# Delta-rule attention with routed experts on one core: a tile for each PSUM bank, unread products that wait for rows, and a new order of all steps

## The chip, the core and the metric

The kernel runs on one core of a Trainium2 chip. Its engines are TensorE (PE, whose weight loads have a row of their own, PEld), VectorE (DVE), ScalarE (ACT), GpSimd (POOL) and SyncE (SP, which here issues most of the DMAs). The metric is the device time of one launch in microseconds (us). The time before is 541.99 us, the median of three runs (534.49, 541.99 and 543.96).

## What is computed

Two parts, one behind the other, all in float32:

```python
# attention, 4 x 8 heads, 768 steps, head size 48: a state of 48 x 48 per head
k_n = k / (norm(k) + 1e-6)
for t in range(768):
    y[t]  = q[t] @ state
    v_old = state.T @ k_n[t]
    state = state + beta[t] * outer(k_n[t], v[t] - v_old)
# experts: y is regrouped to x (3072 x 384); each row goes to one of 8 experts
e_idx  = argmax(x @ w_gate + modality_bias[modality_id])
out[i] = softmax_weight[i] * (relu(x[i] @ w1[e_idx]) @ w2[e_idx])      # hidden size 1024
```

## The kernel before

**Tiling.** The 768 steps are cut into 12 chunks `c` of 64 steps. A chunk has two groups `g` of heads, so there are 24 steps `i` = 2c+g. Within a chunk the recurrence is turned into matrix products: a gram matrix of the keys (`g{c}`, lines 182 to 194, copied out by `ev` and, for the first four chunks, by `dc`), the inverse of a triangular matrix made from it, and products with the state. The inverse is worked out row by row on DVE and POOL in three jobs; the first (`sub0_0` to `sub0_14`, lines 276 to 283) solves blocks of 16 for chunks 0 to 3, and `jy`, `ya`, `jx`, `r1`, `wt`, `mv` (lines 304 to 338) put blocks of 32 together from those of 16, for the eight steps 0 to 7: `jy` and `jx` are products on PE, `ya` copies one's result out for the other, `r1` adds on DVE. Then `y1`, `ys`, `r`, `rc` (lines 398 to 412) make the block of 64.

**The recurrence.** For each step i: `ks` (product of keys and state, line 437), `rh` (DVE subtracts it from the values, 439), `z` (product with the inverse, 443), `zt` (copied out in two halves by ACT or DVE), `ds` (state update in PSUM, 449), `sb` (state copied out), `qs` and `pz` (the output, 457 and 460), `xo` (copied out). Steps of one parity share a state in PSUM, S[0] or S[1].

**PSUM.** Four tiles of two banks each: S (the states), ZK (bank z for `z`, bank ks for `ks`), YG (bank y for `qs` and `pz`, bank gp for `y1`, `r` and small products), MO (two banks handed out to grams, transposes and the first expert's products). Where two engines touch one tile, the framework makes the later wait for the earlier by a semaphore; it does that by tile, so also where they touch different banks, and for two reads too.

**The order.** Every step is a named task of a plan; the string `ORDER` (line 28) lists the tasks in the order in which they are issued, a letter behind a number chooses the engine of a task that has a choice, and `in_order` (line 96) ties each engine to that order. So an engine whose next instruction waits holds up all that stands behind it, SP's DMAs too.

**Unread products.** `hf`, `hg`, `hx` (lines 374 to 379) are 46 products of 128x128 with 128 columns which nobody reads; they go to bank S[1]. Those of `hf` and `hg` are named after rows of the solve. `idle` and `gate` use `issue_after`, which orders instructions only on the engine of the instruction that it names. The rows are DVE's and the gated DMAs SP's, and the named instructions are not on the same engine as the work in the block, so in this kernel neither makes anything wait.

**Experts.** From about 309 us on, PE runs the experts' two layers, unit by unit, from prefetched weights. The first unit's first layer (`la_`, `lh`, `ll`) is part of the plan and stands at its end, on the banks of MO. The change doesn't touch the experts.

Of the kernel before, what the change touches and what calls it, by code (L numbers as in the profile page):

```python
# [49 lines left out]
590d 930d 931 230 991 231 232 233 932 928 933 998 1002 588 941 942 589d 907 904 935 999 934 592 944 936d 992 1000 1001 593 953 596d 908 938 993 955 995 946 945 996 943 594 954  # L50
939 595 909 1003 1004 948 997 1005 949 922 1006 1007 957 951 1008 1009 958 956 1010 1011 1012 952 1013 1014 1015 1016 1017 1020 1021 959 1018 1022 1019 1023 961 415 444 962 964
1024 1025 965 1026 950 966 1027 967 963 989 1028 960 947 968 937 1029"""

FILL="""\
"""

# [49 lines left out]
class Attention:  # L106
# [33 lines left out]
    def plan(s):  # L140
# [261 lines left out]
        def ys(i):  # L402
            t=s.tile("ys",i,[128,8,32],2)
# [647 lines left out]
```

## Time and profile before

| | before |
|---|---|
| time, median of 3 runs | 541.99 us |
| time of the profiled execution | 539.66 us |
| its span, first to last instruction | 537.9 us |
| PE busy | 469.1 us (87%) |
| DVE, ACT, POOL busy | 303.9, 220.8, 136.5 us |
| mean granted clock of TensorE | 0.882 |

The granted clock is a share of 2.4 GHz, and its two levels are 1.0 (2.4 GHz) and 0.5 (1.2 GHz); a value between them is a mean over a stretch. A row of a timeline gives the start, the duration, the engine, the line and what is written from what; "x10" merges ten records. PE leaves two records for a product of float32, so "x10" is five products. Brackets at a row's end name how long the engine had been idle and whose end released it.

### The profile page before, as it was taken

What the parts mean: (1) busy time and instruction counts of PE and PEld (TensorE: products, weight loads), DVE (VectorE), ACT (ScalarE), POOL (GpSimd) and SP (SyncE); (2) the same over time, 40 slices, a digit from 0 to 9 for tenths busy, and PEclk for the clock granted to TensorE, in tenths of its full rate; (3) what the DMA queues carried; (4) which work ended last, traced back from release to release, by engine and by line L of the source; (5) the groups of instructions that cost most, each with busy time, mean ns of one, the idle gap of its engine ahead of it and who ended that gap; (6) DMA issues with size and microseconds to landing.
All of it is one profiled execution on the core that took longest, in us unless ns stands there. A gap on an engine that the chain in (4) does not pass through costs nothing. (4 is left out here: it accounts for less than half of the span.)

```text
span 537.9 us, 16821 instructions
## 1 busy us (share of the span) xinstructions
PE 469.1 (87%) x7119; PEld 414.7 (77%) x7119; DVE 303.9 (56%) x647; ACT 220.8 (41%) x473; POOL 136.5 (25%) x176
## 2 busy tenths in 40 slices
PE   5755998988788897998897799999699999999994
PEld 5645787877667786877685579899489889899984
DVE  3895457497457477557354179955334535444630
ACT  5424344546266456552244263421232424333530
POOL 8007323466333261010300021104412213101121
PEclk9595556688799699997898999999799999999998
DMA  8688004476567376876520384523633533519701
GB/s 270 155 193 271 4 14 114 106 219 189 125 188 177 82 227 191 196 193 167 134 82 16 99 284 132 176 60 104 219 102 103 174 107 98 156 58 327 231 32 35
DMA packets 90628, 78.14 MB, mean 145 GB/s; under 512 B 49049, under 2 KB 78496, under 8 KB 90544
## 3 DMA queue, kind: packets, MB, share of 16 engines
q1 hardware_dynamic: 87408, 67.49, 44.3%
q0 software_dynamic: 3136, 9.49, 5.3%
q8 instruction: 58, 0.95, 0.7%
q14 instruction: 26, 0.21, 0.1%
HBM read 62.28 MB, written 14.73 MB: 143 GB/s over the span
## 5 line engine op out<-in xcount | busy, mean ns | idle before, releaser
L952 PE MATMUL opb<-w2hb,h 128*128 128x384 f32 x192 | 52.9, 340 | 0.5 <-DVE oob L955 0.5
L861 PE MATMUL hpb<-xh,w1xb 128*128 128x512 f32 x144 | 42.1, 405 | 0.6 <-ACT xh L826 0.6
L867 DVE SCALAR_TENSOR_TENSOR h<-hpb,h 128x512 fp32r<-128x512 f32 x24 | 16.6, 692 | 45.5 <-ACT h L865 45.5
L439 DVE TENSOR_TENSOR RHS<-vv,ZK 64x384 f32<-64x384 f32 x44 | 24.3, 551 | 21.6 <-PE ZK L437 6.5
L952 PEld LDWEIGHTS opb<-w2hb,h 128*128 128x128 f32 x192 | 34.8, 188 | 1.8 <-DVE oob L955 1.0
L865 ACT ACTIVATE h<-hpb 128x512 fp32r<-128x512 f32 x24 | 14.4, 598 | 51.0 <-PE hpb L861 51.0
L952 PE MATMUL opa<-w2ha,h 128*128 128x384 f32 x128 | 34.7, 343 | 0.3 <-ACT h L865 0.3
L346 POOL TENSOR_TENSOR tmx<-T,A 128x216 f32<-128x216 f32 (+12 forms) x23 | 18.4, 802 | 63.1 <-DVE T L347 62.5
L952 PE MATMUL opb<-w2lb,h 128*128 128x384 f32 x96 | 32.4, 338 | 0.0
L861 PEld LDWEIGHTS hpb<-xh,w1xb 128*128 128x128 f32 x144 | 27.5, 194 | 5.7 <-ACT xh L826 1.0
L25 ACT COPY Sb<-S 48x192 f32<-48x192 f32 x74 | 23.2, 313 | 18.2 <-PE S L721 6.8
L25 ACT COPY ZT<-ZK 64x384 f32<-64x384 f32 x41 | 19.4, 473 | 23.2 <-PE ZK L437 13.1
L449 PE MATMUL S<-ZT,kk 128*48 128x96 f32 x352 | 24.5, 292 | 4.3 <-issue 2.4
L460 PE MATMUL YG<-ZT,pb 128*64 128x96 f32 x384 | 24.4, 276 | 3.1 <-ACT ZT L25 1.3
L956 POOL DMA_INDIRECT out_dram<-oob,sidxb x12 | 12.2, 1016 | 57.8 <-DVE oob L955 29.5
L443 PE MATMUL ZK<-RHS,R 128*64 128x96 f32 x384 | 25.0, 282 | 1.9 <-DVE RHS L439 1.5
L414 POOL TENSOR_TENSOR vv<-vv,RR 128x384 f32<-128x384 f32 x18 | 15.7, 878 | 40.6 <-DMA kk<-in_kv_dram 26.5
L409 PE MATMUL YG<-R,ys 32*32 32x32 f32 x768 | 20.5, 207 | 5.9 <-issue 2.9
L25 ACT COPY R<-YG 32x256 f32<-32x256 f32 x44 | 15.9, 362 | 23.5 <-PE YG L409 13.5
L409 PEld LDWEIGHTS YG<-R,ys 32*32 32x32 f32 x768 | 17.2, 121 | 10.5 <-issue 4.8
L449 PEld LDWEIGHTS S<-ZT,kk 128*48 128x48 f32 x352 | 19.6, 150 | 6.0 <-issue 3.2
L146 ACT ACTIVATE ys<-YG 32x256 f32<-32x256 f32 x42 | 15.8, 375 | 20.6 <-PE YG L457 6.6
(372 smaller groups left out, 1193.2 us busy)
## 6 DMA issues: line engine op xcount, KB each, us to landing
kqr<-in_kq_dram SPq DMA_DIRECT2D x44, 256.0 KB
ke<-in_kq_dram SPq DMA_DIRECT2D x20, 256.0 KB
vv<-in_kv_dram SPq DMA_DIRECT2D x24, 192.0 KB
xd<-xo SPq DMA_DIRECT2D x24, 192.0 KB
w1rb<-in_moe_w_dram SPq DMA_DIRECT2D x12, 384.0 KB
w2rb<-in_moe_w_dram SPq DMA_DIRECT2D x12, 384.0 KB
kk<-in_kv_dram SPq DMA_DIRECT2D x22, 192.0 KB
w1ra<-in_moe_w_dram SPq DMA_DIRECT2D x8, 384.0 KB
```

Source lines behind the costliest of these rows:

```text
L25: if n=="scalar": nc.scalar.copy(o,i)
L146: if s.e=="ACT": A.activation(o,i,AF.Copy,scale=x)
L346: E[s.e].tensor_tensor(o,T[:,:,lo:lo+na,c:c+1].to_broadcast([128,n,na,nb]),X[:,:,c:c+1,c+1:32].to_broadcast([128,n,na,nb]),ALU.mult)
L409: for p in range(2): b=64*p; x=2*j+h; mm(o[b:b+32,x],s.ys[i][b+32:b+64,x],R[b+32:b+64,x,32:64],start=True,stop=True)
L414: if c: E[s.e].tensor_tensor(v,v,w,ALU.mult)
L439: c,g=divmod(i,2); b=64*p; V.tensor_tensor(s.RHS[g][b:b+64,:,48*p:48*p+48].rearrange("q (h j) c -> q h j c",h=2),s.KV[c,1][b:b+64,g],s.ks[ ...
L443: for h in range(2): mm(s.z[i][64*h:64*h+64,:,j,:],s.R[i%4][:,2*j+h,:],hc(s.RHS[i%2][:,4*h+j,:]),start=True,stop=True)
L449: for p in range(2): mm(o[64*p:64*p+48,j,:],K[:,4*p+j,:],s.ZT[g][:,4*p+j,:],start=False,stop=True,skip_group_check=True)
L460: for p in range(2): mm(s.y[i][64*p:64*p+64,:,j,:],s.PB[i//2][:,8*p+4*(i%2)+j],hc(s.ZT[i%2][:,4*p+j,:]),start=(i<2 and j==0),stop=True,ski ...
L861: if n in ks: mm=s.nc.tensor.matmul(hp[:,v,:],w[:,k,fs],x[:,k,0:T],start=(n==0),stop=(n==8))
L867: s.nc.vector.scalar_tensor_tensor(hl,hp,0.0,hh.bitcast(F32),ALU.max,ALU.subtract)
L952: mm=nc.tensor.matmul(op,h[:,f%nf,ts_],w[:,f%2,:],start=(n==0),stop=(n==23)); n+=1
```

## The change

Five edits, and a new table of numbers for the order of all 1030 tasks:

- **Banks.** The four tiles of two banks become eight tiles of one bank (S0, S1, z, ks, y, gp, MO0, MO1).
- **Unread products** go to bank y, which has no reader until the first `pz`, and must all be issued before `qs0`. Those tied to a row now wait for it by a semaphore (`gate` adds a wait to the first instruction of the block).
- **Gated DMAs.** The same `gate` now makes some early loads on SP wait for the gram products `g1` or `g3`.
- **`ya`** is split by bank: on ACT four instructions of 64 columns in place of two of 128, or two on DVE. The new order puts all eight on ACT.
- **`ys`**: one instruction over 128 rows in place of two over 32 rows (line 402).

```diff
-        S,ZK,YG,MO=(p.tile([128,1024],F32,name=n) for n,p in (("S",s.ps),("ZK",s.ps),("YG",s.ps),("MO",s.pm)))
-        h=lambda t: [t[:,512*g:512*g+512] for g in range(2)]
-        s.S=h(S); s.bk=dict(zip(("z","ks","y","gp"),h(ZK)+h(YG))); s.MO=h(MO); ...
+        B=lambda n,p: p.tile([128,512],F32,name=n)
+        s.S=[B(f"S{g}",s.ps) for g in range(2)]; s.bk={n:B(n,s.ps) for n in ("z","ks","y","gp")}; s.MO=[B(f"MO{g}",s.pm) for g in range(2)]; ...
         def gate(n,f):
-            with s.tc.issue_after(s.I[n].ins): f()
+            k=len(nc.cur_bb.bb.instructions); f(); i=nc.cur_bb.bb.instructions[k]
+            s.tc.add_manual_dep(i,s.I[n].name,mybir.DependencyInfo(mybir.DependencyClass.Sync,mybir.DependencyReason.DATA),reason="gate")
...
                 def ya(i):
-                    for b in range(2): mul(s.ya[:,i%2,:,:,32*b:32*b+16],s.jo[i][:,:,0:128].rearrange("q k (j b a) -> q k j b a",j=4,b=2)[:,:,:,b],s.mk[b])
+                    for p in range(2):
+                        o=s.ya[:,i%2,p].rearrange("q j (b a) -> q j b a",b=2)[:,:,:,0:16]; x=s.jo[i][p][:,0:128].rearrange("q (j b a) -> q j b a",j=4,b=2)
+                        if s.e=="DVE": V.tensor_tensor(o,x,s.cst[:,66:68].unsqueeze(1).unsqueeze(3).to_broadcast([128,4,2,16]),ALU.mult)
+                        else:
+                            for b in range(2): mul(o[:,:,b],x[:,:,b],s.mk[b])
...
         def idle(n,k=None):
-            with s.tc.issue_after(s.I[k]) if k else contextlib.nullcontext():
-                for _ in range(n): mm(s.S[1][:,384:512],s.ident,s.ident,start=2 not in s.gp,stop=True,skip_group_check=True)
-        for c in range(7,15): add(f"hf{c}","PE",.85,lambda c=c: idle(2,f"sub0_{c}"),[f"sub0_{c}","gf2"])
+            def f():
+                for _ in range(n): mm(s.bk["y"][:,384:512],s.ident,s.ident,start=False,stop=True,skip_group_check=True)
+            gate(k,f) if k else f()
+        fy=["gf1","gf5"]; fills=[f"hf{c}" for c in range(7,15)]+["hg0","hg1"]+[f"hx{n}" for n in range(24)]
+        for c in range(7,15): add(f"hf{c}","PE",.85,lambda c=c: idle(2,f"sub0_{c}"),[f"sub0_{c}",*fy])
...
-            for p in range(2): b=64*p+32; mul(t[b:b+32],s.lv[i][b:b+32,0:256].rearrange("q (x c) -> q x c",x=8),-1.0)
+            mul(t,s.lv[i][:,0:256].rearrange("q (x c) -> q x c",x=8),-1.0)
...
 ORDER="""\
-118 3 0 95 130 119 134a 131d 94 152 133d 120 92 93 122 156a 141 237 123 121d 99 155 96 243 124 144 97 98 132 135 1 8 163 101 153 238 2 154 145 239 172 240 164 165 9 112 143 241
+3 118 130 0 95 132d 133d 94 134a 119 93 123 152 131 92 121d 122 237 155 135 243 97 120d 156a 96 98 141 124 99 1 2 102 112 238 144 145 154 163 164 153 239 240 157 165 241 172
```

The order moves instructions in three places of which the prediction speaks.

**VectorE behind the first solve** (T is the solved matrix, W its two transposes, w1b the operand of `jy`, s and tt belong to the second job, A<-W is `r1`). Before:

```order
L285 TENSOR_TENSOR T_354<-T_354,t_450 128x1024 [waits DVE_49]
L288 STREAM_TRANSPOSE W_653<-T_354 128x16x32 [waits DVE_49]
L289 STREAM_TRANSPOSE W_653<-T_354 128x16x32
L288 STREAM_TRANSPOSE W_653<-T_354 128x16x32
L289 STREAM_TRANSPOSE W_653<-T_354 128x16x32
L254 RECIPROCAL tt_798<-s_701 128x64 [waits Activation_49]
```

and after:

```order
L282 TENSOR_TENSOR T_319<-T_319,t_418 128x1024 [waits DVE_49]
L285 STREAM_TRANSPOSE W_682<-T_319 128x16x32 [waits DVE_49]
L286 STREAM_TRANSPOSE W_682<-T_319 128x16x32
L143 TENSOR_SCALAR w1b_172<-W_682,cst 128x32x16 [waits DVE_49]
L285 STREAM_TRANSPOSE W_682<-T_319 128x16x32
L286 STREAM_TRANSPOSE W_682<-T_319 128x16x32
L143 TENSOR_SCALAR w1b_173<-W_682,cst 128x32x16 [waits DVE_49]
L143 TENSOR_SCALAR w1b_173<-W_682,cst 128x32x16
L322 SCALAR_TENSOR_TENSOR A_311<-W_682,cst,z 64x4x16 [waits PE_49,Activation_49]
```

Three of the four copies w1b move from ACT to DVE, and the first `r1` stands ahead of the second job's norm (the RECIPROCAL follows it now).

**ScalarE at the same place.** Before, the second job's square root (s, which waits for two DMAs) stands between the first two copies w1b:

```order
L146 ACTIVATE w1b_168<-W_653,cst 128x32x16 [waits DMAHW1_49,DVE_49]
L250 ACTIVATE s_701<-A_656,eps 128x64 [waits DMAHW5_49,DMAHW2_49]
L146 ACTIVATE w1b_168<-W_653,cst 128x32x16
L146 ACTIVATE w1b_169<-W_653,cst 128x32x16 [waits DVE_49]
L292 ACTIVATE A_339<-W_653,cst 128x32x16 [waits DVE_49,Activation_49]
```

and after, behind the first `ya`:

```order
L142 ACTIVATE w1b_172<-W_682,cst 128x32x16 [waits DMAHW7_49,DVE_49]
L289 ACTIVATE A_311<-W_682,cst 128x32x16 [waits DVE_49,Activation_49]
L142 ACTIVATE ya<-z,cst 128x4x16 [waits PE_49,Pool_49]
L142 ACTIVATE ya<-z,cst 128x4x16
L142 ACTIVATE ya<-ks,cst 128x4x16 [waits PE_49]
L142 ACTIVATE ya<-ks,cst 128x4x16
L247 ACTIVATE s_768<-A_618,eps 128x64 [waits DMAHW6_49,DMAHW4_49]
```

The square root and its wait no longer stand ahead of work that PE waits for. On PE, 16 unread products and 13 groups of small products (`jy`, `jx`, `y1`, `r`) then stand between the first `jy` and the first `z`. Of the ten groups of unread products tied to rows, only two still carry a wait of their own (for `sub0_9` and `sub0_14`); the others stand where their row is long done.

**ScalarE in the recurrence**, at step 19 (ZT is `zt`, R is `rc`, Sb is `sb`, xo is `xo`). Before:

```order
L25 COPY ZT_157<-ZK 64x8x48 [waits DVE_49,PE_49,Activation_49]
L25 COPY R_144<-YG 32x8x32 [waits DVE_49]
L25 COPY R_144<-YG 32x8x32
L25 COPY Sb_161<-S 48x4x48 [waits DVE_49,PE_49,Activation_49]
L25 COPY Sb_161<-S 48x4x48 [waits Activation_49]
```

and after:

```order
L25 COPY ZT_157<-z 64x8x48 [waits PE_49]
L25 COPY ZT_157<-z 64x8x48 [waits Activation_49]
L25 COPY R_144<-gp 32x8x32 x2
L25 COPY xo_4080<-y 128x384 [waits DMAHW6_49,PE_49]
L25 COPY Sb_161<-S_165 48x4x48 [waits PE_49,Activation_49]
```

The waits on VectorE are gone, and the wait on PE is for `z19`, where before it was for `ks20`, a later product in the same tile. Counted over the plan in both programs: `zt` waits for `ks` 11 times before and never after, `zt` for `rh` 20 times and never, `rh` for `zt` 18 and never, `ys` or `rc` for `qs` or `pz` 16 and never, `xo` for `r` or `y1` 10 and never.

## Rows read from the trace of the kernel before

**Rows 1.** The page's first line.

```profile
span 537.9 us, 16821 instructions
```

**Rows 2.** Busy time of the engines in six stretches of the span: the stretch and its length, PE busy (records), PEld, DVE, ACT, POOL, granted clock, DMA share, GB/s.

```profile
0.00:39.30 39.30, 25.54 (x674) 23.45 (x674) 28.06 (x61) 16.59 (x40) 11.24 (x35) 0.83 0.79 211
39.30:69.50 30.20, 22.42 (x552) 20.52 (x552) 15.91 (x42) 11.27 (x28) 14.76 (x21) 0.50 0.39 122
69.50:104.40 34.90, 32.53 (x707) 29.02 (x699) 21.15 (x44) 15.84 (x41) 11.38 (x13) 0.55 0.38 89
104.40:288.70 184.30, 157.35 (x3877) 135.62 (x3876) 114.52 (x243) 94.02 (x231) 54.23 (x62) 0.90 0.59 159
288.70:309.10 20.40, 16.32 (x122) 11.66 (x122) 3.12 (x5) 5.17 (x10) 0.03 (x1) 0.92 0.22 72
309.10:537.90 228.80, 214.95 (x1204) 194.44 (x1202) 121.14 (x255) 77.90 (x124) 44.88 (x45) 0.98 0.45 141
```

**Rows 3.** Timeline of the start, VectorE and (last row) ScalarE: copies of the grams (gk, D) and the two transposes of D.

```profile
7.05 0.69 DVE L26 COPY gk<-ZK 128x512 f32<-128x512 f32 x1 [4.80 <-PE YG L189]
9.76 1.72 DVE L26 COPY D<-ZK 32x256 f32<-32x256 f32 x4 [2.02 <-PE ZK L189]
11.51 1.72 DVE L26 COPY D<-MO 32x256 f32<-32x256 f32 x4
...
13.87 1.93 DVE L244 STREAM_TRANSPOSE A<-D 128x1024 f32<-128x1024 f32 x1
16.34 1.72 DVE L26 COPY D<-S 32x256 f32<-32x256 f32 x4 [0.54 <-ACT D L25]
18.09 1.93 DVE L244 STREAM_TRANSPOSE A<-D 128x1024 f32<-128x1024 f32 x1
...
14.82 1.49 ACT L25 COPY D<-S 32x256 f32<-32x256 f32 x4 [1.23 <-PE S L189]
```

**Rows 4.** Timeline behind the first solve: the first transposes on VectorE, the square root and two copies w1b on ScalarE, the first `jy` on PE.

```profile
38.16 1.03 DVE L288 STREAM_TRANSPOSE W<-T 128x512 f32<-128x512 f32 x1
39.06 1.03 DVE L289 STREAM_TRANSPOSE W<-T 128x512 f32<-128x512 f32 x1
...
43.81 0.41 ACT L250 ACTIVATE s<-A,eps 128x64 f32<-128x64 f32 x1 [3.86 <-DMA A<-GD]
44.12 1.32 ACT L146 ACTIVATE w1b<-W,cst 128x512 f32<-128x512 f32 x2
...
44.89 1.08 PE L309 MATMUL S<-w1b,gk 64*64 64x32 f32 x32 [9.37 <-ACT w1b L146]
```

**Rows 5.** Timeline of the stage from there to the first `z`: on VectorE the first and last part of the second job's norm and an `r1`, on ScalarE two `ya`, on PE unread products and `z0`.

```profile
44.25 0.55 DVE L254 RECIPROCAL tt<-s 128x64 f32<-128x64 f32 x1 [2.41 <-ACT s L250]
...
47.54 2.35 DVE L264 TENSOR_TENSOR A<-A,t 128x1024 f32<-128x1024 f32 x2
...
54.03 1.16 DVE L321 SCALAR_TENSOR_TENSOR A<-W,cst,S 64x64 f32<-64x64 f32 x4 [3.07 <-PE S L376]
...
46.94 0.62 ACT L146 ACTIVATE ya<-ZK,cst 128x128 f32<-128x128 f32 x2 [0.89 <-PE ZK L309]
...
62.66 0.62 ACT L146 ACTIVATE ya<-S,cst 128x128 f32<-128x128 f32 x2 [3.14 <-PE S L376]
...
51.42 2.50 PE L376 MATMUL S<-ident 128*128 128x128 f32 x10
...
69.54 1.55 PE L443 MATMUL ZK<-RHS,R 128*64 128x96 f32 x16
```

**Rows 6.** Timeline of PE, the same kinds of work at both clocks: unread products at 1.0; `jy` at 0.5 and (80.14) at 1.0; a gram and a `z` at 0.5; a `z` at 1.0.

```profile
33.69 1.83 PE L376 MATMUL S<-ident 128*128 128x128 f32 x14
...
45.76 1.06 PE L309 MATMUL ZK<-w1b,gk 64*64 64x32 f32 x32
...
80.14 0.68 PE L309 MATMUL MO<-w1b,gk 64*64 64x32 f32 x32
...
88.72 1.99 PE L189 MATMUL MO<-ke 48*64 48x64 f32 x64
90.63 1.55 PE L443 MATMUL ZK<-RHS,R 128*64 128x96 f32 x16
...
104.36 0.88 PE L443 MATMUL ZK<-RHS,R 128*64 128x96 f32 x16
```

**Rows 7.** Five groups of the view of waits (who waited, for whom: us in total, times, longest), and one copy `zt` of ScalarE in the timeline (step 19).

```profile
ACT ZT L25 <- PE ZK L437: 13.1, 7, 7.6
...
DVE ZT L26 <- ACT ZT L25: 11.0, 3, 5.6
...
ACT ys L146 <- PE YG L457: 6.6, 5, 3.1
...
ACT R L25 <- PE YG L460: 5.5, 4, 2.2
...
DVE RHS L439 <- ACT ZT L25: 5.5, 4, 1.9
...
252.49 0.47 ACT L25 COPY ZT<-ZK 64x384 f32<-64x384 f32 x1 [7.60 <-PE ZK L437]
```

**Rows 8.** Timeline of PE at the first expert's first layer.

```profile
296.35 0.98 PE L861 MATMUL MO<-xh,w1xa 128*128 128x512 f32 x3 [1.79 <-DVE h L867]
...
305.04 0.97 PE L861 MATMUL MO<-xh,w1xa 128*128 128x512 f32 x3 [0.85 <-DVE h L867]
```

More of the change, by code (lines that the diff above doesn't have):

```diff
@@ L50 @@
[L50 to L55, printed above, removed]
+3 118 130 0 95 132d 133d 94 134a 119 93 123 152 131 92 121d 122 237 155 135 243 97 120d 156a 96 98 141 124 99 1 2 102 112 238 144 145 154 163 164 153 239 240 157 165 241 172
@@ L127, in __init__ @@
         s.RHS=ring("RHS",2,[128,8,96],nc.gpsimd); s.ZT=ring("ZT",2,[128,8,96],nc.gpsimd); s.Sb=ring("Sb",2,[112,8,96],nc.gpsimd)
-        S,ZK,YG,MO=(p.tile([128,1024],F32,name=n) for n,p in (("S",s.ps),("ZK",s.ps),("YG",s.ps),("MO",s.pm)))
-        h=lambda t: [t[:,512*g:512*g+512] for g in range(2)]
-        s.S=h(S); s.bk=dict(zip(("z","ks","y","gp"),h(ZK)+h(YG))); s.MO=h(MO); s.mn=0; s.got=None; s.JO=(ZK,S,MO); s.W1b=[s.pk.tile([128,32,32],F32,name=f"w1b{m}",tag=f"gk{10+m}").rearrange("q n (b a) -> q n b a",b=2) for m in range(2)]
+        B=lambda n,p: p.tile([128,512],F32,name=n)
+        s.S=[B(f"S{g}",s.ps) for g in range(2)]; s.bk={n:B(n,s.ps) for n in ("z","ks","y","gp")}; s.MO=[B(f"MO{g}",s.pm) for g in range(2)]; s.mn=0; s.got=None; s.JO=([s.bk["z"],s.bk["ks"]],s.S,s.MO); s.W1b=[s.pk.tile([128,32,32],F32,name=f"w1b{m}",tag=f"gk{10+m}").rearrange("q n (b a) -> q n b a",b=2) for m in range(2)]
         s.D=s.pa.tile([128,2080],F32,name="D",tag="A",bufs=2)[:,0:2048].rearrange("q (m x t) -> q m x t",m=2,x=32)
@@ L188, in gram @@
                             p,h=(e,f) if a else (f,e); u=64*(h^p); x=4*p+j; l=s.KQ[c][u:u+48,g,x,0] if a else s.KE[c][u:u+48,g,x]
-                            s.I[f"g{c}"]=mm(t[e][64*f:64*f+64,64*(4*g+j):64*(4*g+j)+64],l,s.KQ[c][u:u+48,g,x,1] if a else l,start=True,stop=True)
+                            s.I[f"g{c}"]=mm(t[e][64*f:64*f+64,64*(4*g+j):64*(4*g+j)+64],l,s.KQ[c][u:u+48,g,x,1] if a else l,start=True,stop=True).ins
             return t
@@ L374, in idle @@
         def idle(n,k=None):
[L375 to L379 removed]
+            def f():
[3 more added lines that the diff above has]
+        for c in range(7,15): add(f"hf{c}","PE",.85,lambda c=c: idle(2,f"sub0_{c}"),[f"sub0_{c}",*fy])
+        for n,k in enumerate(("fin0","ft0")): add(f"hg{n}","PE",1.3,lambda k=k: idle(3,k),[k,*fy])
+        for n in range(24): add(f"hx{n}","PE",.22,lambda: idle(1),fy)
         def scl(m):
@@ L513, in emit @@
         p=s.plan(); first=len(s.nc.cur_bb.bb.instructions)
-        fill={}
-        for x in FILL.split(): k,n=x.split(":"); n,_,m=n.partition("@"); fill.setdefault(int(k),[]).append((int(n),m))
         free=[0,1]; held={}; of=lambda n: dict(gf="g",pf="pg",xs="xt",le="lg",xl="xp").get(n[:2]) and dict(gf="g",pf="pg",xs="xt",le="lg",xl="xp")[n[:2]]+n[2:] or (f"jy{n[3:]}" if n[:3]=="r1_" else f"la_{n[2:]}_0" if n[:2]=="ll" else "pa")
         for t in p.order():
-            for n,m in fill.get(t["k"],()):
-                with s.tc.issue_after(s.I[m].ins) if m else contextlib.nullcontext():
-                    for _ in range(n): s.nc.tensor.matmul(s.S[1][:,384:512],s.ident,s.ident,start=2 not in s.gp,stop=True,skip_group_check=True)
             if "mo" in t["take"]: s.got=held["pa" if t["name"][:2]=="pa" else t["name"]]=[free.pop(0) for _ in range(t["take"]["mo"])]; s.got=list(s.got)
```

57 lines of the change are left out of this document (29 added, 28 removed).

## The prediction

> **What bounds the kernel now.** I read the page's span first [rows 1], then busy time by stretches [rows 2], then the timeline wherever PE is not full, and last the waits. In [rows 2] the reader is to see three regimes. From 309.10 on PE is busy 214.95 of 228.80 us at a clock of 0.98: these 228.8 us belong to the experts, which the change leaves alone, so whatever is won must be won in the first 309.1 us. From 39.30 to 104.40 PE is busy 54.95 of 65.1 us, but at 0.50 and 0.55, so it runs nearly everything at 1.2 GHz; what it costs there is the number of products times their slow price. From 104.40 to 288.70 PE is busy 157.35 of 184.30 us at 0.90: 27 us without work, and low clock for a fifth of the time (a share x at 0.5 and the rest at 1.0 make 0.90 for x = 0.2), some 37 us.
>
> **The start.** [Rows 3] show VectorE idle 2.02 us before its first D copy and 0.54 us before the last, which waits for ScalarE's D copy of the other half (from 14.82, 1.49 us, so until 16.31). The new order gives VectorE two gk copies more (0.69 each) and lets nothing stand idle ahead of the D copies. Its row of work becomes 0.69+1.72+1.72+0.69+0.69+1.93+1.72, and the second transpose starts when that and the grams are through, which I put at 16.5 us by adding the row to the first gk copy's start at 7.05 (16.2) and some waiting. It started at 18.09: **-1.6 us**. The solve behind it is a chain on VectorE and moves with it. Bounds: 0, if the grams come later, and -1.9.
>
> **From the solve to `z0`.** [Rows 4] show what held the first `jy`: the transposes end at 39.06+1.03 = 40.09, but ScalarE's second copy w1b stands behind a square root that waited 3.86 us for a DMA, and `jy0` starts at 44.89, after 9.37 us of idle PE. In the new order VectorE makes that copy right behind the transposes. No row shows this copy on VectorE; the nearest are its copy of the same size, 0.69 [rows 3], ScalarE's own, 1.32/2 = 0.66, and above them a transpose of that size, 1.03 [rows 4]; I take 0.7. So `jy0` starts at 40.09-1.6+0.7 = 39.2.
>
> From there PE has 13 groups of small products and 16 unread ones. At 0.50 a small group takes 1.06 to 1.08 alone and 0.87 where the next overlaps it (44.89 to 45.76) [rows 4, 6]; I take 0.95. An unread product takes 0.50 (five in 2.50) [rows 5]. 13 x 0.95 + 16 x 0.50 = 20.4 us, so `z0` starts at 59.6, where it stood at 69.54: **-9.9 us**, the start's 1.6 among them.
>
> Is anything else later than PE there? The second job's norm now stands behind the first `r1`. It took from 44.25 to 47.54+2.35 = 49.89, that is 5.6 us [rows 5]. The first `r1` needs `jy`, `ya` and `jx`, so it ends near 44.3; the norm then ends at 49.9, and PE comes to the first `y1`, which needs the `wt` behind it, near 53.6 by the same prices. That leaves 3 us, and it is the cover of two edits that I cost at nothing. The first is the square root's wait (3.86 us [rows 4]), which now holds up only the norm. The second is the gates on SP: a gated load holds back every load queued behind it on SP (the second job's keys, the next chunks', the expert's weights). If those came more than 3 us later than now, the norm, `wt`, `y1` and `z0` would go out one for one. `ya` in four pieces is not in the trace: between the 0.62 of [rows 5] and twice that. I take the upper end and nothing for the time, since other small groups and two unread products fill PE meanwhile. The waits of `r1` and `ya` for unread products (3.07, 3.14 us [rows 5]) go, since these are in another bank than what they read.
>
> **From `z0` to `z3`.** PE then has 11 products of the size of `z` (1.55), 11 small groups (0.95), four grams (1.99) and two unread products (0.50) [rows 5, 6]: 17.1+10.5+8.0+1.0 = 36.5 us at the low clock, against 34.8 now (69.54 to 104.36 [rows 6]). `z3` starts at 96.1 in place of 104.36: **-8 us** for all up to here. Bounds: 0, if the norm or a late load takes it back, and -24 (first rival).
>
> **The recurrence, up to 288.7.** Here the banks work. [Rows 7] give the waits of ScalarE and VectorE for an access to the other bank of a tile: `zt` for the next step's `ks` 13.1 us in 7 times, `ys` for `qs` 6.6, R for `pz` 5.5, RHS for ScalarE's `zt` 5.5, together 30.7. All these go. They don't all lie on the path: one `zt` that stood idle for 7.60 us (252.49) is worth what PE waited for it, and PE has 27 us without work in all. Those that stay are real: VectorE's half of `zt` waits for ScalarE's half of the same bank (11.0 in 3). The page "PSUM — Partial Sum Buffer" of the Trainium skill (section Terms) says why these must: two engines may not be on the same bank and quadrant at once. The trace has that wait and no run without it; the sum here doesn't use it. I take half of PE's idle time as held by these waits, directly or through the order: **-14 us**. Bounds: 0 (nothing of it was on the path) and -40 (all 27 idle us, and most of the low clock's cost: a `z` takes 0.88 at 1.0 and 1.55 at 0.5 [rows 6], so a us of low clock costs 0.43 where PE sets the pace, 37 us at most 16). Both at once is not plausible; -25 is as far as I go. `ys` in one instruction for two saves ScalarE or VectorE one, off the path: nothing.
>
> **The end.** PE waited 1.79 and 0.85 us ahead of products of the first expert because both halves of MO were one tile [rows 8]; that goes, with smaller ones like it: **-3 us**, bounds 0 and -4.
>
> **Sum.** -8-14-3 = -25. The profiled execution took 539.66 us (span 537.9 [rows 1]), which makes 514.7; it lies 2.3 below the median of 541.99, so I forecast **517 us**. Its own range: 507 (recurrence -24) to 529 (recurrence -2).
>
> **Rivals.** (1) *The clock rises in the stage from 39 to 100.* The gap of 9.37 us ahead of `jy0` shrinks, and two groups of unread products really run inside the solve. At 1.0 a small group takes 0.68, an unread product 1.83/7 = 0.26, a `z` 0.88, and a gram by the same ratio 1.13 [rows 6]. PE would then reach `z0` before the norm is through (49.9) and `wt`, `y1`, `ys`, `r` behind it, about 54; and `z3` 11 x 0.88 + 11 x 0.61 + 4 x 1.13 + 0.5 = 21 us later plus some 5 us of waiting, about 80: -24 in place of -8, **501 us**. Against it: PE was busy 22.42 of 30.2 us at 0.50 and 32.53 of 34.9 at 0.55 [rows 2], so being busy with these small products did not raise it. Chance 0.17. The Trainium skill's page "TensorE: Matmul & The Clock Gate" (section What's actually happening) says that throttled is the default and that activity releases it; by that rule the stage should run at 2.4 GHz once PE is kept going, as in this rival; the trace, 0.55 with PE busy 32.53 of 34.9 us, does not agree.
>
> (2) *The waits between banks were not what PE waited for.* An engine that no longer waits early then waits later, for the inverse's rows or a state copy, and the recurrence takes 184 us as before. Then only the start counts, -8: **534 us**, 1.5% less. For it: VectorE and ScalarE are busy only 114.52 and 94.02 of 184.30 us [rows 2], so a late `zt` is often made up; against it, 30.7 us of waits. Chance 0.21.
>
> (3) *Slower: the recurrence loses its clock.* The unread products must now all be issued before `qs0`; behind it nothing fills PE's gaps but work, and it is there that the clock stands at 0.90. If its low share went from 20 to 60% of 184 us, 74 us more at 0.4 us each, that is +29 in place of -14: 539.7-8-3+29+2.3 = **560 us**. It decides from 27 us more of low clock (27 x 0.4 = 11, what the start and end give), with nothing won by the banks. Against it: only some ten unread products stood behind that point before, and real work of 157.35 us is the bulk. Chance 0.10.
>
> That the unread products don't do what their names say is part of the forecast: eight of ten groups tied to rows come after their row anyway and cost 0.50 each.
>
> **How the numbers follow.** Forecast 0.52, rivals 0.17, 0.21, 0.10. The range from 498 to 535 takes in the forecast, (2), and most of (1); it leaves out (3) and the far end of (1), under 0.2. Two per cent, about what a measurement of this kernel can tell from no change, is 531.2 and 552.8: faster are the forecast and (1), 0.69; within it (2), 0.21; slower (3), 0.10.
>
> **What would show it.** In the profile after: the second transpose near 16.5, `jy0` near 39, `z0` near 60 and `z3` near 96, all at about 0.5; if `z0` is right and PE idles ahead of `y1`, the norm or a gated load is late. No wait of `zt` for `ks`; PE's idle time between `z3` and the experts about half of 27 us at a clock of 0.9 (below 0.75 it is the third rival; idle as before, the second). The experts start near 284. The forecast is wrong if that start moves by less than 10 us, or if the experts themselves take other than 229 us.

## The result and the profile after

The changed kernel takes 501.05 us (median of 4 runs, 497.21 to 503.51) where the kernel before took 540.33 in the same runs: 0.930 of it, with a 95% interval of 0.919 to 0.941. The profiled execution took 500.99 us. Its page begins:

```profile
span 499.3 us, 16815 instructions
```

The span is 38.6 us shorter than that of [rows 1]. Where they went is read from the view of windows, cut at `z0`, `z3`, `z23` and the experts' first product on a bank of their own, for PE alone (length, PE busy, records, granted clock, DMA share, GB/s):

```profile
0.00:60.76 60.76, 50.59 (x1196) 0.71 0.75 208
60.76:88.11 27.35, 25.62 (x808) 0.78 0.32 73
88.11:253.75 165.64, 150.34 (x3802) 0.90 0.65 179
253.75:272.51 18.76, 16.30 (x133) 0.91 0.68 205
272.51:499.28 226.77, 213.38 (x1197) 0.98 0.42 132
```

The same stretches of before are 69.54, 34.82, 184.30, 20.40 and 228.82 us long. So 8.8 us come from the way to `z0`, 7.5 from `z0` to `z3`, 18.7 from the recurrence behind it, 1.6 from the end and 2.1 from the experts.

The second transpose on VectorE, the first copy w1b there, and the norm of the second job behind the first `r1`, which answer to [rows 3 to 5]:

```profile
17.33 1.95 DVE L241 STREAM_TRANSPOSE A<-D 128x1024 f32<-128x1024 f32 x1
...
39.24 0.43 DVE L143 TENSOR_SCALAR w1b<-W,cst 128x512 f32<-128x512 f32 x1
...
45.23 0.55 DVE L251 RECIPROCAL tt<-s 128x64 f32<-128x64 f32 x1
45.82 0.67 DVE L251 TENSOR_TENSOR tt<-tt,A 128x64 f32<-128x64 f32 x1
46.52 0.81 DVE L251 TENSOR_TENSOR tt<-tt,s 128x64 f32<-128x64 f32 x1
...
50.11 2.35 DVE L261 TENSOR_TENSOR A<-A,t 128x1024 f32<-128x1024 f32 x2
52.38 0.44 DVE L325 STREAM_TRANSPOSE Wt<-A 128x256 f32<-128x256 f32 x1
```

ScalarE and PE at the same place (the square root waited for its load; the last unread products of the solve; the first `y1` and `z0`):

```profile
44.25 0.41 ACT L247 ACTIVATE s<-A,eps 128x64 f32<-128x64 f32 x1 [2.32 <-DMA A<-GD]
```

```profile
36.18 3.36 PE L377 MATMUL y<-ident 128*128 128x128 f32 x14 [2.60 <-DVE T L278]
...
54.05 1.06 PE L404 MATMUL gp<-Wt,gk 32*32 32x32 f32 x32
...
60.76 1.55 PE L446 MATMUL z<-RHS,R 128*64 128x96 f32 x16
```

The first small product starts at 39.82. The clock stays at 0.50 from there to 72 and rises then; the view of windows, 2 us each, PE alone:

```profile
70.00:72.00 2.00, 2.00 (x48) 0.50 0.28 50
72.00:74.00 2.00, 2.00 (x60) 0.80 0.40 147
74.00:76.00 2.00, 1.24 (x73) 1.00 0.03 8
...
88.00:90.00 2.00, 0.66 (x20) 0.97 0.95 180
90.00:92.00 2.00, 1.04 (x14) 0.50 0.29 63
```

So the stretch from `z0` to `z3` is shorter though it has more work: 808 records, where the kernel before has 703 (and 3802 behind it, for 3875). What went ahead of the loss at 90 is told where the prediction is compared. In the view of waits ScalarE's `zt` now waits for its own product `z`; the 13.1 us of [rows 7] for `ks` are gone:

```profile
ACT ZT L25 <- PE z L446: 8.5, 11, 3.0
```

### The profile page after: what moved, and what is told of

It is laid out like the page before. It is cut to its first block, busy times and chain, and to the rows that moved or that the text cites. A ratio compares the mean times of both kernels' runs of the same rounds, so it can differ in the third digit from the quotient of the medians.

```text
span 499.3 us, 16815 instructions
## 1 busy us (share of the span) xinstructions
PE 456.2 (91%) x7119; PEld 407.8 (82%) x7119; DVE 304.1 (61%) x644; ACT 214.4 (43%) x469; POOL 139.3 (28%) x175
## 5 line engine op out<-in xcount | busy, mean ns | idle before, releaser
L950 PEld LDWEIGHTS opb<-w2hb,h 128*128 128x128 f32 x192 | 34.8, 188 | 1.8 <-DVE oob L953 1.0
L859 PEld LDWEIGHTS hpb<-xh,w1xb 128*128 128x128 f32 x144 | 27.8, 196 | 10.2 <-ACT xh L824 5.3
L442 DVE TENSOR_TENSOR RHS<-vv,ks 64x384 f32<-64x384 f32 x44 | 24.2, 551 | 19.0 <-PE ks L440 14.1
L25 ACT COPY Sb<-S 48x192 f32<-48x192 f32 x76 | 23.8, 313 | 25.2 <-PE S L452 16.8
L347 POOL TENSOR_TENSOR tmx<-T,A 128x300 f32<-128x300 f32 (+12 forms) x25 | 20.7, 829 | 43.8 <-DVE T L348 42.9
L446 PE MATMUL z<-RHS,R 128*64 128x96 f32 x384 | 23.9, 272 | 3.5 <-issue 2.3
L463 PE MATMUL y<-ZT,pb 128*64 128x96 f32 x384 | 25.8, 282 | 1.1 <-issue 1.1
L950 PEld LDWEIGHTS opa<-w2ha,h 128*128 128x128 f32 x128 | 23.6, 193 | 0.8 <-DVE ooa L953 0.2
L186 PE MATMUL MO<-kqr 48*64 48x64 f32 x832 | 17.9, 229 | 6.7 <-DMA kqr<-in_kq_dram 4.1
L194 DVE TENSOR_TENSOR pb<-MO,cst 128x512 f32<-128x512 f32 x24 | 15.5, 685 | 13.9 <-PE MO L186 13.8
L25 ACT COPY R<-gp 32x256 f32<-32x256 f32 x46 | 16.7, 362 | 16.8 <-PE gp L412 16.3
L347 DVE TENSOR_TENSOR tmx<-T,A 128x368 f32<-128x368 f32 (+14 forms) x35 | 22.0, 628 | 3.1 <-POOL T L348 2.1
L463 PEld LDWEIGHTS y<-ZT,pb 128*64 128x64 f32 x384 | 20.4, 157 | 4.0 <-issue 3.2
```

The lines of the kernel that those rows point to most:

```text
L25: if n=="scalar": nc.scalar.copy(o,i)
L186: s.I[f"g{c}"]=mm(t[e][64*f:64*f+64,64*(4*g+j):64*(4*g+j)+64],l,s.KQ[c][u:u+48,g,x,1] if a else l,start=True,stop=True).ins
L194: V.tensor_tensor(s.PB[c][:,8*p:8*p+8],s.pp[c][p].rearrange("q (x t) -> q x t",x=8),s.um.unsqueeze(1).to_broadcast([128,8,64]),ALU.mult)
L347: E[s.e].tensor_tensor(o,T[:,:,lo:lo+na,c:c+1].to_broadcast([128,n,na,nb]),X[:,:,c:c+1,c+1:32].to_broadcast([128,n,na,nb]),ALU.mult)
L442: c,g=divmod(i,2); b=64*p; V.tensor_tensor(s.RHS[g][b:b+64,:,48*p:48*p+48].rearrange("q (h j) c -> q h j c",h=2),s.KV[c,1][b:b+64,g],s.ks[ ...
L446: for h in range(2): mm(s.z[i][64*h:64*h+64,:,j,:],s.R[i%4][:,2*j+h,:],hc(s.RHS[i%2][:,4*h+j,:]),start=True,stop=True)
```

## The experiments

Twelve runs were made, in three sets of four, each set on one chip beside the kernel before; two of the twelve repeat a kernel. The experts' part, which no edit touches, took 226 to 230 us in the profiles of before, of after and of the second set, and 218 to 222 in the first and third. So single profiles are compared up to the experts' start, and the whole by the ratio to the kernel before on the same chip. The kernel before has one profile only; two profiles of one kernel (after, and none in stage) differ by up to 3 us in a stretch. Lengths in us:

| | to `z0` | `z0` to `z3` | `z3` to `z23` | end | experts start | ratio (95%) |
|---|---|---|---|---|---|---|
| before | 69.5 | 34.8 | 184.3 | 20.4 | 309.1 | 1 |
| after | 60.8 | 27.4 | 165.6 | 18.8 | 272.5 | 0.930 (0.919 to 0.941) |
| after again | 60.5 | 27.3 | 162.8 | 16.4 | 267.0 | 0.926 (0.916 to 0.936) |
| banks only | 68.0 | 26.6 | 166.0 | 15.0 | 275.6 | 0.936 (0.927 to 0.945) |
| after, two-bank tiles | 63.7 | 28.5 | 178.9 | 26.5 | 297.5 | 0.975 (0.961 to 0.988) |
| only z, ks apart | 70.8 | 27.6 | 174.4 | 20.9 | 293.6 | 0.986, of medians |
| all but z, ks apart | 68.6 | 29.5 | 174.1 | 15.0 | 287.2 | 0.962 (0.955 to 0.969) |
| rows in solve | 57.9 | 29.6 | 159.4 | 16.8 | 263.7 | 0.914 (0.900 to 0.929) |
| none in stage | 56.1 | 28.2 | 160.5 | 18.7 | 263.5 | 0.898 (0.887 to 0.910) |
| none in stage, again | 55.3 | 31.0 | 160.4 | 16.4 | 263.0 | 0.918 (0.907 to 0.928) |
| none at all | 55.3 | 28.9 | 161.9 | 16.5 | 262.6 | 0.917 (0.910 to 0.924) |
| both and `wt0` | 54.9 | 27.7 | 160.7 | 16.9 | 260.2 | 0.914 (0.899 to 0.930) |
| no row waits | 61.0 | 29.0 | 162.6 | 18.3 | 270.9 | 0.936 (0.928 to 0.944) |
| banks, none in stage | 62.3 | 25.5 | 169.7 | 15.0 | 272.4 | 0.934 (0.924 to 0.944) |

The run with only z and ks apart spread from 517.03 to 536.43 us (median 529.35, before 536.69) and has no interval; its profile is of an execution of 523.53 us. `ZK`, `YG` and the like in the lines below are the old tiles of two banks, `z`, `ks` and so on the new ones of one.

**Banks or order?** The theory of the prediction is that the waits between banks hold PE; the rival, that the order does. One kernel has the banks alone, in the old order:

```diff
-        S,ZK,YG,MO=(p.tile([128,1024],F32,name=n) for n,p in ...)
+        s.S=[B(f"S{g}",s.ps) for g in range(2)]; s.bk={n:B(n,s.ps) for n in ("z","ks","y","gp")}; s.MO=[B(f"MO{g}",s.pm) for g in range(2)]; ...
```

(shortened; `ya` in one piece per bank belongs to it, as in the changed kernel).

> The kernel before with one edit: eight tiles of one bank (and ya in one piece per bank, which they need); its order, its unread products and its loads stay. If the waits between banks held PE, the recurrence gives most of what it gave: the last z some 10 to 14 us earlier, 526 to 531 us. If the gain is the order's, since engines that no longer wait early wait later for what the old order puts ahead of them, it is 536 us or more, and PE's idle time from 112.8 to 288.7 stays near 26.6 us.

It takes 499.26 us (0.936), nearly all of the gain, and lower than the theory had said (526 to 531); some 7 us of that are the experts on that chip (221.9 for 228.8 us). Its windows from `z0` on:

```profile
67.97:94.56 26.59, 24.70 (x703) 0.79 0.42 101
94.56:260.58 166.02, 150.79 (x3875) 0.92 0.66 179
260.58:275.60 15.02, 13.72 (x122) 1.00 0.30 93
```

Between `z3` and `z23` PE does the same 3875 records in the same order as before, 11.7 us less idle (166.02-150.79 = 15.2 for 27.0) and 6.6 us less busy (150.79 for 157.35 [rows 2]). The clock there is 0.92 for 0.90, which makes some 10 us less at half the clock (37 for 27); at the prediction's 0.43 us for each that is an estimate of 4.4 of the 6.6 us. Waiting as such didn't vanish: ScalarE's `zt` waits 14.2 us for its own `z`, where before it waited 13.1 for `ks`, 3.7 for `rh` and 3.5 for `z`. That PE stands idle less is what shows that the old waits were on its path. The other kernel is the changed one with the old tiles, the same edit the other way round.

> The changed kernel with one edit undone: four tiles of two banks; the new order, the waits for rows and the gated loads stay. If the gain is the order's alone, 503 to 508 us. If the new order counts on banks that don't wait for each other, each wait comes back in a place where something now stands behind it: 515 to 530 us, with idle time of PE in the recurrence near 26 us again.

519.76 us. The new order on the old tiles wins 6 us on the way to `z0`, as much again to `z3`, 5 in the recurrence, and loses 6 at the end:

```profile
92.12:271.03 178.91, 152.07 (x3802) 0.90 0.61 166
271.03:297.50 26.47, 20.53 (x147) 0.87 0.66 209
```

PE's idle time in the recurrence is back at 26.8 us, as its second case had it. Then one kernel took only z and ks apart, the other all but these (here the second, against the banks-only kernel, shortened):

```diff
-        ... s.bk={n:B(n,s.ps) for n in ("z","ks","y","gp")}; ...
+        ZK=s.ps.tile([128,1024],F32,name="ZK"); ... s.bk=dict(z=ZK[:,0:512],ks=ZK[:,512:1024],y=B("y",s.ps),gp=B("gp",s.ps)); ...
```

> The kernel before with only one of its four tiles taken apart, the one with the banks z and ks; S, YG and MO stay tiles of two banks. By the waits of the trace (zt for ks 13.1 us, RHS for zt 5.5, of 30.7 in all, and the 1.41 us without work at 82.4 us after which the clock fell) it brings more than half of what all eight tiles bring: 0.95 to 0.965. If the waits inside YG (ys for qs, R for pz, 12.1 us) hold PE instead, 0.975 or more.

> The kernel before with S, YG and MO taken apart and z and ks left in one tile: the other half of the run in which only z and ks were taken apart (0.985). If the two halves add, 0.945 to 0.955, since all eight gave 0.936. If either half alone leaves the other's waits to hold PE, so that only both together bring the gain, 0.97 or more.

Each brings about half in the recurrence (-9.9 and -10.2; both -18.3), so by the stages these waits add up, and "more than half" for z and ks was too much. The ratios are less clear: 0.962 lies between its two cases, and 0.986, by the medians, falls into the second of its own. The end's 5.4 us come with MO apart: with only z and ks apart PE still waits 1.79 and 0.85 us there as in [rows 8], in the other kernel no such wait is left. From `z0` to `z3` the two kernels differ in clock: 27.6 us with z and ks apart, clock 0.80; 29.5 with them together, clock 0.62:

```profile
70.75:98.33 27.58, 24.51 (x702) 0.80 0.42 100
```

```profile
68.60:98.14 29.54, 28.78 (x703) 0.62 0.36 84
```

What happens there is seen in the timeline of the kernel before: ScalarE's two halves of `zt1`, and PE's state update `ds1` that waits for them:

```profile
81.82 0.47 ACT L25 COPY ZT<-ZK 64x384 f32<-64x384 f32 x1 [0.96 <-PE ZK L437]
83.29 0.47 ACT L25 COPY ZT<-ZK 64x384 f32<-64x384 f32 x1 [1.00 <-DVE RHS L439]
```

```profile
83.81 1.52 PE L449 MATMUL S<-ZT,kk 128*48 128x96 f32 x16 [1.41 <-ACT ZT L25]
```

The first half waits for `ks2`, the second for VectorE's reading of `ks2`, both in the other bank; PE stands idle 1.41 us, and the clock, which had just risen, falls right behind that. Windows of before, and then of the banks only at the same step:

```profile
80.00:82.00 2.00, 2.00 (x70) 0.94 0.78 194
82.00:84.00 2.00, 0.59 (x28) 0.91 0.90 308
84.00:86.00 2.00, 2.00 (x44) 0.50 0.02 6
```

```profile
80.00:82.00 2.00, 2.00 (x77) 1.00 0.71 253
82.00:84.00 2.00, 1.78 (x77) 1.00 0.72 163
```

with `zt` in one go and `ds1` without a wait:

```profile
78.38 0.96 ACT L25 COPY ZT<-z 64x384 f32<-64x384 f32 x2
```

With only z and ks together the two waits are there again, at the same step, but there the clock had not risen yet and does so only at 91:

```profile
80.87 0.47 ACT L25 COPY ZT<-ZK 64x384 f32<-64x384 f32 x1 [1.89 <-PE ZK L441]
81.96 0.47 ACT L25 COPY ZT<-ZK 64x384 f32<-64x384 f32 x1 [0.61 <-DVE RHS L443]
```

So in the old order the low clock from `z0` to `z3` goes with z and ks in one tile, in two profiles of each kind. It is not the wait alone that does it. In the new order on the old tiles a wait of the same kind is there: ScalarE's half of a `zt` waits 1.40 us for VectorE's reading of the other bank, VectorE's half comes behind it, and PE stands idle 1.14 us ahead of its state update. The clock stays (ScalarE, PE, then windows):

```profile
82.27 0.47 ACT L25 COPY ZT<-ZK 64x384 f32<-64x384 f32 x1 [1.40 <-DVE RHS L443]
```

```profile
83.39 0.87 PE L453 MATMUL S<-ZT,kk 128*48 128x96 f32 x16 [1.14 <-DVE ZT L26]
```

```profile
82.00:84.00 2.00, 0.86 (x33) 1.00 0.48 76
84.00:86.00 2.00, 2.00 (x68) 1.00 0.65 131
```

That stretch takes 28.5 us at 0.78 with two-bank tiles. So either the banks or the new order is enough to shorten it, by one profile each.

**Yardstick.**

> The changed kernel once more, unedited, as a yardstick on the chip of the next three. If the banks alone (0.936 in their run) are all of the gain, 0.93 to 0.94 of the kernel before; if the new order adds to them what the stages say (z0 7 us earlier, but z4 1 us later than with the banks alone, the recurrence behind it 8 us shorter, the end 4 us longer), it is 1 to 2% below the banks alone, 0.915 to 0.925.

0.926, between its two cases. By stages the order adds to the banks what was read: 7 us on the way to `z0`, 0 to 3 us in the recurrence, and it gives back 0.7 us from `z0` to `z3` and 1.4 to 3.7 at the end. By the ratios (0.926 and 0.930 against 0.936) it is not clear of noise, as long as the unread products are in.

**Do the unread products pay?** Four kernels move them or leave them out.

The first leaves out the 18 between the first `jy` and the first `qs` (`hf8`, `hf10` to `hf12`, `hg0`, `hg1` and four `hx`; the line of `hf` is shown):

```diff
-add(f"hf{c}","PE",.85,lambda c=c: idle(2,f"sub0_{c}"),[f"sub0_{c}",*fy])
+add(f"hf{c}","PE",.85,lambda c=c: idle(2 if c in (7,9,13,14) else 0,f"sub0_{c}"),[f"sub0_{c}",*fy])
```

> The changed kernel without the 18 unread products issued between the first jy and the first qs0 (those in and ahead of the solve stay). If they only cost their 0.50 us each, z0 comes up to 8 us earlier, or about 2 to 4 us where the norm (through at 52.4 in the changed kernel) is then later than PE: 494 to 499 us. If they are what brings the clock up at 72.8, it stays at 0.5 until about 104, z3 comes at 94 or later in place of 88.1, and the time is 503 to 510 us.

> The changed kernel without the 18 unread products of the stage once more, as a yardstick on the same chip: 0.89 to 0.91 of the kernel before, if the first run of it was no exception; 0.92 to 0.93 if it was, and the unread products then cost nothing.

`z0` comes at 56.1 and 55.3 (60.8 and 60.5 in the two profiles of the changed kernel), the experts at 263.5 and 263.0 (272.5 and 267.0): 4 to 5 us and 3.5 to 9.5 us earlier. The first run's 482.59 us lie below both of its cases, 7 us of that in the experts on that chip; its ratio is 0.898. The second's is 0.918, between its two cases and nearer to the one in which they cost nothing. So they cost their time up to `z0`, a little more than the 2 to 4 us that the first case allowed beside the norm. Whether they bring the clock is not settled. In the first run it rises at 70, earlier than with them (72 in both profiles), but in the second run of the same kernel only at 80:

```profile
68.00:70.00 2.00, 2.00 (x46) 0.50 0.19 68
70.00:72.00 2.00, 1.24 (x64) 0.92 0.03 8
```

```profile
80.00:82.00 2.00, 2.00 (x93) 0.97 0.61 95
```

So one kernel's clock rises 10 us apart in two executions, and in neither as late as the 104 of the case in which they bring it. The next moves five groups of them into the solve instead, each behind its row (PE's list of tasks, shortened):

```diff
 hf9
+hf10
+hf11
+hf12
+hf13
 hf14
 hx20
-hf13
 hf7
+hg0
 jy0
-hf11
 jy1
...
```

> The changed kernel with five groups of unread products (hf10 to hf13, hg0) moved on PE: from behind the first jy to the solve, behind the rows that they are named after, so that PE no longer stands idle 2.60 us ahead of hf14. Theory that the clock is lost there: it stays at 1.0 up to the first jy, small products take about 0.6 us each, z0 comes at 55 to 57 in place of 60.8 and the time is 489 to 497 us. Rival, that small products lose the clock by themselves or while PE waits for the norm: clock 0.5 again from about 45 on, z0 at 57 to 59, only the 3.5 us of moved products are won, 496 to 500 us.

The hole ahead of `hf14` is closed, and the clock is at 1.00 at the first small product; it is lost right behind it all the same:

```profile
38.00:40.00 2.00, 0.87 (x60) 1.00 0.81 221
40.00:42.00 2.00, 1.70 (x52) 0.61 0.94 286
42.00:44.00 2.00, 1.37 (x30) 0.50 0.94 250
```

That is the rival of its expectation: the clock is not held through the small products, `z0` comes at 57.9. The hole doesn't decide either: the changed kernel's second profile has it (2.31 us without work ahead of `hf14`), and its clock too is full at the first small product and lost behind it:

```profile
40.00:42.00 2.00, 1.76 (x67) 0.97 0.93 245
42.00:44.00 2.00, 1.79 (x30) 0.50 0.83 279
```

The 488.18 us of the kernel with the moves are lower than the rival's 496 to 500, 7 us of it in the experts on that chip. Then none of the 46 at all:

```diff
-            gate(k,f) if k else f()
+            pass
```

> The changed kernel without any of its 46 unread products; the gated loads stay gated. If those in and ahead of the solve buy something, the early grams run at 0.5 from about 14 on to the solve's end, and z0 comes 1 to 3 us later than without the stage's alone (56.1): 0.90 to 0.91. If no unread product is worth anything, since the clock is lost at 36 or at the first jy either way, it is the same as without the stage's: 0.895 to 0.90.

484.23 us, 0.917: the same as without the stage's alone on that chip (0.918). The clock is at 0.61 up to `z0` for 0.73, and `z0` stands at 55.3 in both; in the solve it is VectorE's chain that counts, so the unread products ahead of it win nothing. In the old order with one bank to a tile, the 22 from the first small product on are left out:

```diff
-for n in range(24): add(f"hx{n}","PE",.22,lambda: idle(1),["gf2"])
+for n in range(24): add(f"hx{n}","PE",.22,lambda n=n: idle(int(n in (15,23,0,5,4,14,16,10,22,7,20,8))),["gf2"])
```

(and `hf7`, `hf9`, `hf10`, `hf12`, `hg0` likewise).

> The kernel before with one bank to a tile (as in the run with the banks only) and without its 22 unread products from the first jy on; the old order. If the new order is worth nothing once the banks are apart, it comes where the changed kernel without its unread products came, 0.90 to 0.91 of the kernel before. If the old order needs them, or is the worse one, 0.925 or more. 12 of them stand ahead of z0 at 0.50 us each: z0 at 62 to 64 in place of 68.0.

0.934 (0.924 to 0.944), no better than the banks alone: the second case. `z0` comes 5.7 us earlier, but from `z3` to `z23` it is 3.6 us longer at 0.89 for 0.92, where seven of the unread products had stood. Whether these held the clock there is one profile's word only. But without the unread products the new order is ahead of the old one: the experts start at 262.6 to 263.5 (three profiles) for 272.4, and the ratio is 0.898, 0.918 and 0.917; the intervals of the last two just touch this one's.

**The waits for rows and loads.** `gate` does nothing here, for unread products and loads alike:

```diff
-        def gate(n,f):
-            k=len(nc.cur_bb.bb.instructions); f(); i=nc.cur_bb.bb.instructions[k]
...
+        gate=lambda n,f: f()
```

> The changed kernel without the waits that gate adds: unread products wait for no row, gated loads for no gram. If the waits are worth nothing, 0.99 to 1.01 of the changed kernel, with hf14 some 2.6 us earlier and the clock lost ahead of the first jy as now. If the gated loads come late through their gates (the square root waited for its load until 44.25, the norm ran to 52.4), the norm is through 2 to 3 us earlier and z0 comes 1 to 2 us earlier, 0.995. If loads without gates get in the way of the early grams, the second transpose comes later than 17.33 by 1 us or more.

499.81 us against 494.49 on the same chip; the intervals overlap. The square root's load is there at 41.3 in place of 44.2, so the gates do make it 3 us late, and the norm is through 2.4 us earlier (50.1 for 52.5). But `z0` stands at 61.0: with PE busy nearly all the way from the first small product on (21.35 of 21.99 us, and 20.94 of 20.94 with the gates), an earlier norm wins nothing. The second transpose came at 16.50, not later than with the gates, so the third case fell too.

**A version put together**: the moves into the solve as above, the rest of the stage's unread products left out, and VectorE's list changed:

```diff
 r1_0
+wt0
 n1
 sc1
-wt0
```

> A version put together from what the runs showed: the changed kernel without the unread products that cost time in the stage (hf8, hg1 and four hx left out), with hf10 to hf13 and hg0 in the solve, and with the first wt moved on VectorE ahead of the second job's norm. If the norm is what PE waits for there (wt0 ended at 52.82 behind it), z0 comes at 53 to 54 in place of 56.1 and the time is 1% below the run without them, 0.885 to 0.895 of the kernel before. If z0's other inputs are as late (the product on GpSimd that fills RHS ran to 49.0), nothing is won: 0.895 to 0.905.

486.09 us (0.914), above both of its cases. `wt0` ahead of the norm brings `z0` to 54.9, 0.4 to 1.2 us ahead of the kernels without unread products in the stage. The norm holds PE all the same, by another way: the next `r1` stands behind it on VectorE (from 49.88, the norm's last product ends at 49.85), and a `jy` waits for that `r1`:

```profile
51.10 1.08 PE L307 MATMUL S<-w1b,gk 64*64 64x32 f32 x32 [1.07 <-DVE A L323]
```

All five runs with fewer or earlier unread products in the new order (four kernels) start the experts at 260.2 to 263.7, ahead of 267.0 and 272.5 in the changed kernel, and their medians are 482.6 to 488.2 us. By the ratio only the first of them (0.898) is clear of the changed kernel's intervals, and among themselves they can't be told apart.

## Why the prediction was right, and where its sum was not

The direction was right and 501 lies in the range, but the sum said -25 us and the span lost 38.6. Point by point:

| | forecast | measured |
|---|---|---|
| second transpose | 16.5 | 17.33 |
| first small product | 39.2 | 39.82 |
| `z0` | 59.6 | 60.76 |
| `z0` to `z3` | 36.5 | 27.35 |
| `z3` to `z23` | 170.3 | 165.64 |
| end | 17.4 | 18.76 |

**The start and the stage** held to 1.2 us. VectorE made its row of copies without a gap but began it 1.3 us later (8.36 for 7.05), waiting for the first gram. The copy w1b took 0.43 on VectorE, not 0.7. PE was busy 20.94 of 20.94 us from the first small product to `z0`, at 0.50, as priced. Of the 3 us of cover that I had named 1.2 were left: the gates made the square root's load 3 us late, the norm took 7.2 us (45.23 to 52.46), not 5.6, and `wt0` behind it ended at 52.82; PE reached `y1` at 54.05.

**From `z0` to `z3`** is the step that failed: "PE then has 11 products of the size of `z` (1.55), 11 small groups (0.95), four grams (1.99) [...] at the low clock". I priced all of it at the low clock, because before the stretch ran at 0.55 with PE busy 93% of the time. But that mean over 34.8 us hid that the clock had risen at 80 and was lost 4 us later, behind a wait between banks; [rows 6] even show the `jy` of 80.14 at 1.0. In the changed kernel it rose at 72 and was kept up to `z3`: 27.35 us for 36.5, with 808 records. The banks alone keep it (26.6 us at 0.79), the new order on the old tiles does so too (28.5 at 0.78, in spite of a wait of the same kind). So what failed is the premise that this work stays at the low clock, and with it a term of 36.5 us that measured 27.35; why the clock was lost in the kernel before and not in those two is open. Rival 1 gave 26 us to this stretch, near the 27.35 measured, but for another reason: up to `z0`, where it also saw 2.4 GHz, the clock stayed at 0.50.

**The recurrence** had the right mechanism and was sized too small: -14 forecast, -18.7 measured, -18.3 by the banks alone. The idle time fell by 11.7 us, near the half of 27 that I took; that it was half and not more was a guess, and lucky. What I left to the bounds is PE's busy time: the same records took 6.6 us less with the banks apart, an estimated 4.4 of it by the clock. In the changed kernel PE was busy 7.0 us less at the same clock of 0.90, with 73 records fewer. Less idle time does not by itself bring a higher clock there: PE stood idle 23.3 us at 0.93 with only z and ks apart, 19.4 at 0.88 with all but these, 15.3 at 0.90 in the changed kernel. And one wait that I called real did not stay: VectorE's half of `zt` for ScalarE's, 11.0 us in 3 times before, is 0.4 in one time after; the sum didn't use it.

**The end**: -3 forecast. The banks alone give -5.4; the new order has more work there and keeps 1.6 to 4.0 of it.

**Rival 2**, that the waits between banks are not on the path, fell with the banks-only kernel. **Rival 3**, the loss of the clock behind the last unread product, did not come: 0.90 and 0.93 from `z3` to `z23`. That the unread products cost 0.50 us each was part of the sum and right; that `z0` would come 4 to 5 us earlier without them was not weighed.

What stays open: one execution of the changed kernel lost its clock from 90 to 103 when PE stopped 2.31 us inside `z3`, waiting for nothing that the profile shows, and came to `z4` at 104.2; the other profiled one did not stop and came at 96.0. What stopped it was not tried.

## What to carry to other kernels

Two banks in one tile make engines wait for each other where they need not; taking them apart cost four smaller copies in place of two here. The place to look for it is a copy whose releaser works on a different bank than the copy reads, and the test is whether the idle time of the bounding engine falls, since the waits themselves may only change their names. Before a low clock is taken as given for a stretch, cut the stretch into windows of 2 us: a mean can hide a clock that rises and is lost again, and then the whole stretch is priced wrongly. One profile doesn't settle when the clock rises: two executions of one kernel here were 10 us apart. Products that nobody reads are to be tested by leaving them out; here `z0` came 4 to 5 us and the experts 3.5 to 9.5 us earlier without them, and no gain from them could be told from the spread of executions.

## What the chip showed beside that

**A busy PE at half the clock.** From 39.82 to 60.76 PE was busy all the time at 0.50, with products of 64 x 64 and 32 x 32 and unread ones between them; the clock rose at 72. In the kernel with the rows in the solve it was full at 39 and lost within 2 us of the first small product. The Trainium skill's "TensorE: Matmul & The Clock Gate" (section What's actually happening) has activity release the clock; 20.94 us without a gap at 0.50 don't agree with that as it stands.

**Length alone doesn't say which gap loses the clock.** 1.41 us without work went ahead of the loss in the kernel before, at 82.40; 1.14 us did not lose it in the new order on the old tiles. In the first run without the stage's unread products PE stood still 1.96 us, and the clock stayed (windows, then the timeline of PE):

```profile
86.00:88.00 2.00, 0.12 (x7) 1.00 0.45 70
88.00:90.00 2.00, 1.92 (x45) 1.00 0.59 140
```

```profile
88.08 0.53 PE L404 MATMUL gp<-Wt,gk 32*32 32x32 f32 x22 [1.96 <-issue]
```

How a gap loses the clock is not shown here.

**VectorE is slower while GpSimd works.** In the second job's norm two products of 128x64 took 0.67 and 0.81 us, from 45.82 on, while GpSimd ran four products of its own:

```profile
45.52 3.52 POOL L419 TENSOR_TENSOR RHS<-vv,RR 64x384 f32<-64x384 f32 x4 [3.42 <-DMA vv<-in_kv_dram]
```

In the first job's norm, with no record of GpSimd between 17 and 24, the same two are

```profile
20.34 0.28 DVE L251 TENSOR_TENSOR tt<-tt,A 128x64 f32<-128x64 f32 x1
20.66 0.22 DVE L251 TENSOR_TENSOR tt<-tt,s 128x64 f32<-128x64 f32 x1
```

So it is with a TENSOR_SCALAR and a product behind them (0.84 and 0.89 for 0.20 and 0.23), while the RECIPROCAL took 0.55 in both. Against the second job's norm of before, where the four took 0.38, 0.37, 0.20 and 0.23, they are 2.0 us longer; a later product went the other way (0.67 before, with GpSimd at work from 46.49, and 0.23 after). That makes the norm's 1.6 us above my 5.6. The Trainium skill's "GPSIMD Engine Reference" (section 1. Specifications) lists the access to SBUF as shared with VectorE, in contention with instructions of two inputs among others; the rows of the two products agree.
